# Sliding-window attention and soft mixture of experts on one core: warm products, half loads, moved constants, banks and spreads

## Chip, core and metric

The kernel runs on one core of one Trainium2 chip. The metric is the device time of one execution in microseconds (us). TensorE (PE) multiplies matrices, VectorE (DVE) and ScalarE (ACT) work elementwise, GpSimd (POOL) copies and issues the loads, SyncE (SP) issues the output's transfers.

## What is computed

The input is q, k and v in 8 batches of 8 heads, with 576 positions of 64 values each, and the weights of a soft mixture of 8 experts with 4 slots each. Each position attends to itself and to the 63 positions before it. The result, as 4608 rows of 512 values, goes through the mixture:

```python
scores = q @ k.T / sqrt(64)                      # per batch and head
mask = (rel >= 0) & (rel < 64)                   # rel = query position - key position
attn = softmax(where(mask, scores, -1e9))
x = (attn @ v) reshaped to (4608, 512)

logits = x @ phi                                 # phi: 512 x 32
d = softmax of logits over the 4608 rows         # dispatch
slot_input = d.T @ x                             # 32 x 512
slot_out[e] = relu(slot_input[e] @ w1[e]) @ w2[e]   # w1: 512 x 1024, w2: 1024 x 512
c = softmax of logits over the 32 slots          # combine
out = c @ slot_out
```

## The kernel before

**Attention.** Two heads make a pair, so there are 32 pairs, 4 to a batch. The loop `for n in range(-1, NP - 1)` has one slot for each n, and in a slot several pairs stand at different stages: the maxima of pair n - 1 (`st_max`, `st_max8`), the products with v of pair n - 3 (`st_av`, L329) and their normalization (`st_norm`, L338 and L339), the turning of pair n's q and pair n + 1's k (`st_transpose`, L256) with the copies that scale them (L263, L268), the scores of pair n - 2 (`st_score`, L305 and L307) with their exponential (L312; block 8 by itself, L318), and the shift that carries the maxima into the next products (`st_shift`, L299 and L300). The order of every engine is written out by hand; the program follows it.

**Mixture, front.** Four pairs complete a batch. The functions `fr_*` then make its logits, a running maximum (L377, L379), the exponential (L393), the dispatch weights turned (`fr_dispatch`, L439) and copied (`fr_dispatch_copy`, L444 and L445), and add to the accumulator acc (`fr_acc`, L462). In the loop this is spread over slots 8 to 11 after the batch's first pair; the dispatch of a batch stands in slots 10, 14, 18, 22, 26 and 30, after `st_norm`. The functions `cb_*` make the combine weights: maximum, difference (on GpSimd, L410), exponential (L416), sum (L422), product (on GpSimd, L430) and turning into `ct_all` (L435).

**Loads.** All loads of q, k, v and the expert weights are cast to 16 bits on the way and issued by GpSimd, in an order laid down by `loads(n)`. Each load has one of eight semaphores, so it is issued only once the load eight places before it has landed. Between the loads GpSimd shifts v by 64 positions (`shift_v`, L160 and L162), which `st_av` reads.

**Memory for products.** TensorE writes to five tiles of the accumulator memory: `a_m`, `a_v` and `a_s` of two banks each, `a_k` and `a_q` of one. The block 8 of a pair's maxima, `m8`, lies in `a_v`; that of its scores, `s8`, in `a_k`.

**Tail.** After the loop the last two pairs and batches are written out step by step. `fill(k, bank)` issues k products whose results are not used. The sums over all batches give a factor `fac`, and acc times `fac` is turned by products with `ss` into the slot inputs `sit` (L664, L665, L668, L672). `first(g, f2)` is a half of the first expert products (L692), `turn_hidden` turns the hidden values (L707), `second(g, fcs)` is the second product (L713) into `op`. `spread(b, copy)` brings the combine weights of batch b into the layout that the output needs, by five products (L733) and one copy (L736). All eight spreads stand before the output loop: 0 to 5 among the expert products, 6 and 7 behind them.

**Output.** 13 turns of one to three rows per partition: products (L796), a copy by ScalarE or VectorE in turn (L797), and a transfer by SyncE (L799).

Of the kernel before, what the change touches and what calls it, by code (L numbers as in the profile page):

```python
# [18 lines left out]
def kernel(  # L19
# [10 lines left out]
    nc = tc.nc  # L30
# [33 lines left out]
    nc.vector.memset(a_q[:, 448:512], -1.0e30)  # L64
# [11 lines left out]
    def load_rows(src, g, tag):  # L76
        t = pin.tile([128, 4, RQ * Dh], FP16, name=tag, tag=tag)
        b, gq = divmod(g, 2)
        nc.gpsimd.dma_start(out=t[0:RP], in_=src[b].rearrange("h (p r) d -> p h (r d)", p=RP)[:, 4 * gq:4 * gq + 4, :])  # L79
        staged[tag, g] = t  # L80
# [82 lines left out]

    load_k(1)
# [11 lines left out]
    qbs = [pqk.tile([128, NB, 2, 64], FP16, name=f"qb{i}") for i in range(NQ)]  # L176
    for t_ in kTs:
        nc.vector.memset(t_[:, 0:64], 0.0)
    for t_ in qbs:
        nc.vector.memset(t_[64:128, :, 0, :], 0.0)  # L180
        nc.vector.memset(t_[0:64, :, 1, :], 0.0)
# [6 lines left out]
    nc.vector.tensor_copy(out=db[64:128, 11:12], in_=ident_h[64:128, 64 + NB:65 + NB])  # L188
    wm = const.tile([128, 5, 128], FP16, name="wm")
# [4 lines left out]
    lh = const.tile([128, NB, 128], FP16, name="lh")  # L194
    nc.vector.tensor_copy(out=lh[0:64], in_=wb[:, :].unsqueeze(1).broadcast_to([64, NB, 128]))
    nc.vector.tensor_copy(out=lh[64:128], in_=db[64:128, 0:NB].unsqueeze(2).broadcast_to([64, NB, 128]))
    nc.vector.tensor_tensor(out=lh[64:128, 0, 0:64], in0=lh[64:128, 0, 0:64],
                            in1=db[64:128, 10:11].broadcast_to([64, 64]), op=ALU.add)
    NR = 2
    rts = [const.tile([128, 128], FP16, name=f"rt{i}") for i in range(NR)]  # L200
    for rt in rts:
        nc.vector.tensor_copy(out=rt[64:128, :], in_=db[64:128, 11:12].broadcast_to([64, 128]))
        nc.vector.tensor_copy(out=rt[0:64, 0:64], in_=ident_h[0:64, 0:64])
        nc.vector.tensor_copy(out=rt[0:64, 64:128], in_=ident_h[0:64, 0:64])
    for i in range(2):
# [14 lines left out]
    def late_constants(part):  # L220
        if part == 1:
            nc.vector.tensor_copy(out=phi_sb, in_=phi_f)
            nc.vector.memset(quarter, 0.0)
            for t in range(4):
# [4 lines left out]
            return  # L229
        nc.vector.tensor_copy(out=ssf, in_=ss)  # L230
        nc.vector.memset(emask, 0.0)
        for g in range(2):
# [10 lines left out]
    nc.vector.memset(nmax[1], 1.0e30)  # L243
    nc.vector.memset(stat, 0.0)
# [6 lines left out]
    def st_transpose(p, tag, tq):  # L251
        src = staged[tag, p // 2]
        h = 2 * (p % 2)
# [11 lines left out]
    def st_copy_q(p):  # L265
        for hf in range(2):
            h = slice(64 * hf, 64 * hf + 64)
            nc.scalar.activation(qbs[p % NQ][h, :, hf, :], turned(a_qh)[h], AF.Copy, scale=QKS)  # L268
# [28 lines left out]
    def st_shift(p):  # L297
        t_ = (a_v if p < NP - 1 else a_m)[64:64 + NB, 1, 384:512]
# [197 lines left out]
    for n in range(-1, NP - 1):  # L496
# [57 lines left out]
        if n in (1, 2):  # L554
            late_constants(n)
# [15 lines left out]

    b, p = B - 1, NP - 1
    loads(NP - 1)
    m8_last = a_k[:, 0:128]
    st_max(p - 1)
    st_max8(p - 1)
# [4 lines left out]
    st_max8_read(p - 1)  # L581
    cb_exp(b - 3)
    st_copy_q(p)
    st_av(p - 3)
    st_norm(p - 3)
    st_score(p - 2)
    st_scores(p - 2, (8,), lambda i: s8)
    st_exp8(p - 2)
    fr_transpose(p - 4)
    fr_transpose_copy(p - 4)  # L590
    st_shift(p - 1)
    st_max(p)
    st_max8(p, m8_last)
    st_max8_read(p, m8_last)
# [4 lines left out]
    st_shift(p)  # L599
# [32 lines left out]
    fill(4, a_v[:, 1, :])  # L632
# [17 lines left out]
    fill(2, a_v[:, 1, :])  # L650
# [6 lines left out]
    fill(5, a_m[:, 1, :])  # L657
    fac = pmo.tile([128, 1], FP32, name="fac")
    nc.vector.reciprocal(fac, mg[:, 4:5])
    nc.vector.tensor_tensor(out=fac, in0=fac, in1=wt, op=ALU.mult)  # L660

    accs = [kTs[i][:, 0:256].rearrange("p (c x) -> p c x", c=2) for i in range(2)]
    accv = acc[:, :].rearrange("p (x c) -> p c x", c=NKK)
    nc.vector.tensor_scalar(out=accs[0], in0=accv[:, 0:2, :], scalar1=fac[:, :], scalar2=None, op0=ALU.mult)  # L664
    nc.scalar.activation(accs[1], accv[:, 2:4, :], AF.Copy, scale=fac[:, :])  # L665
    sit_ps = a_q[:, 0:128].rearrange("p (c s) -> p c s", s=32)
    for kk in range(NKK):
        nc.tensor.matmul(sit_ps[:, kk, :], accs[kk // 2][:, kk % 2, :], ss[:, 0, :], start=True, stop=True,  # L668
                         skip_group_check=True)
    fill(2, a_m[:, 1, :])  # L670
    sit = pmo.tile([128, NKK, 32], FP16, name="sit")
    nc.scalar.copy(out=sit, in_=sit_ps)  # L672
    patt.close()
    pex = ExitStack()
# [35 lines left out]
    def second(g, fcs):  # L710
        for fc in fcs:
# [5 lines left out]

    NE = 2 * S // 128
    ct4 = [v1s[0][:, 12 * i:12 * i + 12, :].rearrange("p c x -> p (c x)").rearrange("p (e x) -> p e x", e=NE)
           for i in range(3)]  # L720
    ct4.append(v2s[0][:, :, :].rearrange("p c x -> p (c x)")[:, 0:2 * S].rearrange("p (e x) -> p e x", e=NE))

    ss4 = qbs[2][:, 0:4, :, :].rearrange("p t l x -> p t (l x)")
# [104 lines left out]
```

## Time and profile before

| | us |
|---|---|
| median of 3 runs | 205.19 (204.86 to 205.47) |
| profiled execution | 204.57 |
| its span, first to last instruction | 202.5 |
| TensorE busy in the span | 167.7 (83%) |
| ScalarE busy | 141.2 (70%) |
| VectorE busy | 139.4 (69%) |
| GpSimd busy | 100.4 (50%) |

HBM read was 61.93 MB and written 9.44 MB. Busy time is that of an engine's own instructions; matrix products overlap, so a busy TensorE is not one at its peak. A row of the timeline gives start, duration, engine, line, operation, what it writes and reads, and in brackets the idle time of its engine before it with what ended it. Lines are those of the kernel before.

### The profile page before, as it was taken

The page shows a single profiled execution, that of the slowest core. Times are in us where ns is not written, and L with a number is a line of the kernel's source. Part 1 is how long each engine was busy: PE and PEld are TensorE (multiplying, and loading weights), DVE is VectorE, ACT ScalarE, POOL GpSimd, SP SyncE. Part 2 cuts the span into 40 slices and gives each one's busy share as a digit, 9 for nine tenths or more (in the row PEclk, how much of TensorE's full clock was granted, in tenths as well). Part 3 has the DMA queues.
Part 4 walks back from the last instruction along what each step waited for, and adds up shares of the span by engine and source line. Part 5 has one row for each costly group of instructions (what it writes and reads, how often), then busy time and mean ns, then how long its engine had stood idle before and what let it go on. Part 6 is the DMA issues. An engine that isn't in the chain of part 4 may idle for free.

```text
span 202.5 us, 6749 instructions
## 1 busy us (share of the span) xinstructions
PE 167.7 (83%) x2921; PEld 120.1 (59%) x2921; DVE 139.4 (69%) x328; ACT 141.2 (70%) x255; POOL 100.4 (50%) x127
## 2 busy tenths in 40 slices
PE   0699799989999999999999999999799999555200
PEld 0368677767677677767767776776684355221000
DVE  6878765768676767968777796877677768366300
ACT  2447688879688878969887996988677364465300
POOL 7957837473829655693938674683620024000000
PEclk9999999999999999999999999999999999999965
DMA  5999999999999999999999999999999700199994
GB/s 67 183 182 201 205 199 204 182 205 193 212 190 207 190 213 184 190 210 190 209 187 211 190 211 186 194 208 197 210 214 211 153 18 0 52 394 404 416 419 183
DMA packets 56429, 40.87 MB, mean 202 GB/s; under 512 B 38736, under 2 KB 51024, under 8 KB 55504
## 3 DMA queue, kind: packets, MB, share of 16 engines
q0 software_dynamic: 54000, 30.94, 108.5%
q1 hardware_dynamic: 2400, 9.50, 11.7%
q8 instruction: 23, 0.38, 0.7%
q14 instruction: 6, 0.05, 0.1%
HBM read 61.93 MB, written 9.44 MB: 352 GB/s over the span
## 4 chain that ended last, share of the span: by engine, by line
PE 47%; ACT 18%; DVE 17%; issue 7%; DMA 3%; POOL 2%; DVEq 0%; ACTq 0%; POOLq 0%
ACT qb L268 6%; DVE m L284 6%; PE a_m L279 5%; PE a_m L282 5%; ACT pt L312 4%; PE a_q L256 4%; DVE w L797 4%; PE a_q L353 4%; PE a_s L305 3%; PE a_k L256 3%; PE a_s L307 3%; PE a_v L329 3%; PE cp L796 3%; DMA qs<-in_q_dram 3%; ACT kT L263 2%
## 5 line engine op out<-in xcount | busy, mean ns | idle before, releaser
L268 ACT ACTIVATE qb<-a_q 64x576 f16<-64x576 f16 x64 | 41.2, 644 | 19.6 <-PE a_q L256 19.1
L284 DVE TENSOR_REDUCE m<-a_m 128x8 f16<-128x1024 f32 x32 | 39.2, 1224 | 13.1 <-PE a_m L282 12.6
L312 ACT ACTIVATE pt<-a_s 128x1024 f16<-128x1024 f32 x32 | 32.7, 1023 | 3.3 <-PE a_s L307 2.5
L339 DVE TENSOR_TENSOR x_b<-a_v,rc 128x640 f16<-128x640 f32 x31 | 25.6, 824 | 1.1
L263 ACT ACTIVATE kT<-a_k 128x576 f16<-128x576 f16 x32 | 21.0, 655 | 4.9 <-PE a_k L256 4.8
L153 POOL DMA_DIRECT2D v<-in_v_dram x16 | 19.8, 1235 | 7.5 <-DMA ks<-in_k_dram 5.9
L282 PEld LDWEIGHTS <-qb 128*128 128x128 f16 x256 | 17.6, 101 | 8.6 <-ACT qb L268 1.3
L357 ACT COPY xt<-a_q 128x576 f16<-128x576 f16 x31 | 20.5, 660 | 0.2 <-PE a_q L353 0.2
L307 PEld LDWEIGHTS <-kT 128*128 128x128 f16 x288 | 19.1, 99 | 2.2 <-issue 2.1
L282 PE MATMUL a_m<-kT,qb 128*128 128x128 f16 x256 | 20.4, 225 | 0.0
L305 PE MATMUL a_s<-rt,lh 128*128 128x128 f16 x256 | 20.2, 223 | 0.0
L279 PE MATMUL a_m<-wm,ident_h 128*128 128x512 f16 x64 | 20.2, 399 | 0.0
L256 PE MATMUL a_k<-ident_h,ks 96*64 96x96 f16 x384 | 15.0, 217 | 6.1 <-DMA ks<-in_k_dram 6.1
L307 PE MATMUL a_s<-qb,kT 128*128 128x128 f16 x256 | 19.8, 221 | 0.0
L160 POOL COPY v<-v 64x1152 f16<-64x1152 f16 x16 | 18.2, 1140 | 2.7 <-DMA v<-in_v_dram 2.0
L79 POOL DMA_DIRECT2D qs<-in_q_dram x16 | 11.1, 691 | 16.9 <-PE a_q L256 6.7
L300 DVE CAST rt<-a_v 9x128 f16<-9x128 f32 x31 | 9.0, 289 | 15.0 <-PE a_v L299 14.9
L305 PEld LDWEIGHTS <-lh 128*128 128x128 f16 x288 | 17.9, 99 | 1.8
L162 POOL COPY v<-v 64x1088 f16<-64x1088 f16 (+1 forms) x16 | 17.9, 1118 | 0.8
L256 PE MATMUL a_q<-ident_h,qs 96*64 96x96 f16 x384 | 15.3, 214 | 2.8 <-DMA qs<-in_q_dram 0.8
L329 PE MATMUL a_v<-v,pt 128*64 128x65 f16 x558 | 15.6, 197 | 1.9 <-DVE m L295 1.0
L256 PEld LDWEIGHTS <-ks 96*64 96x64 f16 x384 | 10.7, 115 | 9.9 <-DMA ks<-in_k_dram 6.1
(154 smaller groups left out, 312.5 us busy)
## 6 DMA issues: line engine op xcount, KB each, us to landing
w<-in_moe_w_dram POOLq DMA_DIRECT2D x13, 1024.0 KB, 18.5
out_dram<-w SPq DMA_DIRECT2D x11, 768.0 KB, 7.9
ks<-in_k_dram POOLq DMA_DIRECT2D x16, 288.0 KB, 16.0
qs<-in_q_dram POOLq DMA_DIRECT2D x16, 288.0 KB, 15.4
v<-in_v_dram POOLq DMA_DIRECT2D x16, 288.0 KB, 17.3
w2h<-in_moe_w_dram POOLq DMA_DIRECT2D x4, 256.0 KB, 15.9
w1h<-in_moe_w_dram POOLq DMA_DIRECT2D x4, 256.0 KB, 17.9
w<-in_moe_w_dram POOLq DMA_DIRECT2D x2, 512.0 KB, 15.1
```

Of the source, the lines that this page charges most:

```text
L256: nc.tensor.transpose(tq[64 * hf:64 * hf + 64, RP * r:RP * r + RP], src[0:RP, h + hf, Dh * r:Dh * r + Dh], ident_h[0:RP, 0:RP])
L263: nc.scalar.activation(kTs[p % NK][:, 64:64 + S], turned(a_kh), AF.Copy, scale=QKS)
L268: nc.scalar.activation(qbs[p % NQ][h, :, hf, :], turned(a_qh)[h], AF.Copy, scale=QKS)
L279: nc.tensor.matmul(a_m[:, j, :], ident_h[:, :], wm[:, j:j + 4, :].rearrange("p c x -> p (c x)"), start=True, stop=False, skip_group_check= ...
L282: nc.tensor.matmul(a_m[:, i // 4, 128 * (i % 4):128 * (i % 4) + 128], qblock(p, i), kwindow(p, i), start=False, stop=True, skip_group_chec ...
L284: nc.vector.reduce_max(m[:, 0:8].rearrange("p (l c) -> p l c", l=2), a_m[:, :, :].rearrange("p l (c x) -> p l c x", x=128), axis=AXX)
L305: nc.tensor.matmul(at(i), lh[:, i, :], rt[:, :], start=(i % 4 == 0), stop=False, skip_group_check=True)
L307: nc.tensor.matmul(at(i), kwindow(p, i), qblock(p, i), start=False, stop=True, skip_group_check=True)
L312: nc.scalar.activation(pt[:, 0:8, :].rearrange("p i x -> p (i x)"), a_s[:, :, :], AF.Exp, scale=XS)
L329: nc.tensor.matmul(a_v[r0:r0 + 64, hf, 65 * (i // 2):65 * (i // 2) + 65], pt[:, i, 64 * hf:64 * hf + 64], rhs, start=True, stop=True, skip ...
L339: nc.vector.tensor_tensor(out=xbs[b][:, :, 128 * hp:128 * hp + 128].rearrange("p c (l d) -> p l c d", l=2), in0=avv[:, :, :, 0:64], in1=rc ...
L357: nc.scalar.copy(out=xts[b][:, hp, :], in_=a_qh[:, 0:S])
```

## The change

- `warm_up` issues products of a tile of ones, 10 before the first turning and 6 in slot 0; their results are not used.
- The first group's k and q, loaded as two pairs in one transfer, are loaded one pair a transfer. The second pair's q goes behind the mask constants on GpSimd, and the memset of `wb` moves from VectorE to GpSimd.
- Constants that VectorE made before the loop or in slots 1 and 2 move into slots 1, 2, 5, 7, 15, 19 and 23; two parts of `lh` are made by ScalarE. In pair 0 VectorE makes one of the two copies of q.
- `fr_dispatch` and its copies stand before `st_norm`.
- In the tail, block 8 of the maxima of the last two pairs lies in `a_k`, the shift of pair 30 too, and the steps between are reordered.
- Spreads 0 and 1 stand where a fill product stood in the mixture's tail; 2 and 3 stay among the expert products; 4 to 7 stand in the output loop after turns 4, 6, 8 and 9. Their constant `ss4` is made by GpSimd.
- acc times `fac` is written in acc's own order, in two contiguous halves, and the products read it at stride 4. `op` and the first output row are copied half by ScalarE and half by VectorE.

```diff
-    load_k(0)
-    load_q(0)
+    load_rows(k, 0, "ks", (0,))
+    load_rows(q, 0, "qs", (0,))
     ident_h = const.tile([128, 128], FP16, name="ident_h")
     make_identity(nc, ident_h)
+    load_rows(k, 0, "ks", (1,))
     wb = const.tile([64, 128], FP16, name="wb")
-    nc.vector.memset(wb, 0.0)
+    nc.gpsimd.memset(wb, 0.0)
...
+    warm = v1s[1][:, 0:7, :].rearrange("p c x -> p (c x)")
+    nc.vector.memset(warm, 1.0)
+    def warm_up(n):
+        for i in range(n):
+            nc.tensor.matmul(a_m[:, i % 2, :], warm[:, 0:128], warm[:, 128:640], start=True, stop=True,
+                             skip_group_check=True)
+    warm_up(10)
+    load_rows(q, 0, "qs", (1,))
...
+    def late_constants(n):
+        if n == 1:
+            zero_q(2)
+            ones_v(0)
+        elif n == 2:
+            ones_v(1)
+        elif n == 5:
             nc.vector.tensor_copy(out=phi_sb, in_=phi_f)
...
+        elif n == 7:
             for t in range(4):
                 nc.vector.tensor_copy(out=ss[32 * t:32 * t + 32],
...
+        elif n == 15:
+            nc.vector.tensor_copy(out=ssf, in_=ss)
+            nc.vector.memset(emask, 0.0)
+        elif n in (19, 23):
+            g = n // 4 - 4
             for j in range(4):
...
-        if live(n - 3):
-            st_norm(n - 3)
         if live(n):
             st_transpose(n, "qs", a_qh)
             st_copy_q(n)
+        if n == 0:
+            masks_by_key()
+            warm_up(6)
         if sb is not None:
             fr_dispatch(sb)
             fr_dispatch_copy(sb)
+        if live(n - 3):
+            st_norm(n - 3)
+        if sb is not None:
             fr_stat(sb)
...
-    st_max8(p - 1)
+    st_max8(p - 1, m8k)
     st_transpose(p, "qs", a_qh)
     load_last1()
     shift_v(NG - 1)
     load_w(2 * NRES - 1)
-    st_max8_read(p - 1)
+    make_ss4()
+    st_max8_read(p - 1, m8k)
     cb_exp(b - 3)
     st_copy_q(p)
     st_av(p - 3)
+    st_score(p - 2)
+    st_shift(p - 1, a_k[64:64 + NB, 128:256])
     st_norm(p - 3)
...
-    fill(4, a_v[:, 1, :])
+    spread(0, nc.scalar.copy, a_vf)
+    fill(3, a_k[:, :])
...
-    fill(2, a_v[:, 1, :])
+    spread(1, nc.scalar.copy, a_mf)
+    fill(1, a_v[:, 1, :])
...
-    nc.vector.tensor_scalar(out=accs[0], in0=accv[:, 0:2, :], scalar1=fac[:, :], scalar2=None, op0=ALU.mult)
-    nc.scalar.activation(accs[1], accv[:, 2:4, :], AF.Copy, scale=fac[:, :])
+    nc.vector.tensor_scalar(out=accs[:, 0:256], in0=acc[:, 0:256], scalar1=fac[:, :], scalar2=None, op0=ALU.mult)
+    nc.scalar.activation(accs[:, 256:512], acc[:, 256:512], AF.Copy, scale=fac[:, :])
...
-    nc.scalar.copy(out=osb, in_=op[:, :])
-    cb_turn(b)
-    spread(6, act)
-    spread(7, dve)
+    cb_turn(b)
+    act(out=osb[:, 0:256], in_=op[:, 0:256])
+    dve(out=osb[:, 256:512], in_=op[:, 256:512])
...
+            if turn == 0:
+                act(out=ob[:, 0, 0:256], in_=cp[:, 0, 0:256])
+                dve(out=ob[:, 0, 256:512], in_=cp[:, 0, 256:512])
...
+            if turn in (4, 6, 8, 9):
+                spread((4, 6, 8, 9).index(turn) + 4, (act, dve)[turn % 2])
```

More of the change, by code (lines that the diff above doesn't have):

```diff
@@ L192, with masks_by_key, ones_v @@
     nc.vector.memset(wm[:, 0, 0:64], NEG)
[L194 to L205, printed above, removed]
+    make_rt(rts[1])
+    def masks_by_key():
+        nc.scalar.copy(out=lh[0:64], in_=wb[:, :].unsqueeze(1).broadcast_to([64, NB, 128]))
+        nc.vector.tensor_tensor(out=lh[64:128, 0, 0:64], in0=lh[64:128, 0, 0:64],
+                                in1=db[64:128, 10:11].broadcast_to([64, 64]), op=ALU.add)
+    def ones_v(i):
         nc.vector.memset(v1s[i][:, :, Dh:Dh + 1], 1.0)
@@ L715, in second @@
                                  stop=(g == 1 and fc == NFC - 1), skip_group_check=True)
[L718 to L723, printed above, removed]
[L724 to L737 removed]
     act, dve = nc.scalar.copy, nc.vector.tensor_copy
     first(0, 0)
+    fr_turn(b)
+    cb_max(b - 2)
+    cb_sub(b - 2, nc.gpsimd)
     cb_turn(b - 4)
[L742 to L743 removed]
+    cb_sum(b - 3)
+    cb_mul(b - 3, nc.gpsimd)
     first(0, 1)
[L745 to L746 removed]
+    cb_max(b - 1)
+    cb_sub(b - 1, nc.gpsimd)
     first(1, 0)
     turn_hidden(0)
[L749 to L756 removed]
     cb_exp(b - 2)
@@ L759 @@
     cb_sub(b, nc.gpsimd)
+    first(1, 1)
+    second(0, range(4))
     cb_sum(b - 2)
     turn_hidden(1)
+    spread(2, act)
     cb_mul(b - 2, nc.gpsimd)
+    cb_turn(b - 3)
     cb_exp(b - 1)
-    cb_turn(b - 3)
+    second(0, range(4, 8))
     spread(3, act)
-    second(0, range(4, 8))
     cb_sum(b - 1)
@@ L770 @@
     cb_turn(b - 2)
-    spread(4, act)
-    second(1, range(4))
+    second(1, range(8))
     cb_sum(b)
```

129 lines of the change are left out of this document (66 added, 63 removed).

## The prediction

> **What bounds the kernel now.** I read the page first, then the waits, the chain in order of time, and the timeline around each place the change touches.
>
> ```profile
> span 202.5 us, 6749 instructions
> q0 software_dynamic: 54000, 30.94, 108.5%
> ```
>
> The profiled execution took 204.57 us, so 2.07 us lie around its span. The queue of GpSimd's loads moved 30.94 MB, and its packets took 108.5% of sixteen engines' whole span although loads run for only four fifths of it. The engines are therefore full from the first loads to the last, and a load lands when the bytes ahead of it are through, not when a buffer is free.
>
> ```profile
> PE a_v L329 <- POOL v L162: 0.6, 1, 0.6
> DVE m L284 <- PE a_m L282: 12.6, 23, 0.7
> ```
>
> Behind its load issues GpSimd shifts v (L160, L162), and TensorE once stood 0.6 us at L329 for that shift. What holds GpSimd itself, and how close another slot comes, the timeline shows:
>
> ```profile
> 104.18 0.74 POOL L79 DMA_DIRECT2D qs<-in_q_dram  x1 [2.98 <-DMA w<-in_moe_w_dram]
> 104.97 1.14 POOL L160 COPY v<-v 64x1152 f16<-64x1152 f16 x1
> 106.17 1.09 POOL L162 COPY v<-v 64x1088 f16<-64x1088 f16 x1
> ...
> 107.61 0.47 PE L329 MATMUL a_v<-v,pt 128*64 128x65 f16 x17
> ```
>
> A weight's landing releases the q load at 104.18, the shift ends at 107.26, and L329 needs it at 107.61. So whatever is gained before this slot, no more than 0.35 us of it passes. I call this the pin. The change leaves the bytes and GpSimd's order as they are.
>
> After the loop the chain runs through TensorE, ScalarE and VectorE up to the first output; from there the output's own transfers set the end:
>
> ```profile
> 178.00:200.00 22.00, 6.71 (x27) 2.43 (x26) 8.29 (x5) 7.19 (x5) 0.00 (x0) 0.87 1.00 406
> ```
>
> The DMA share is 1.00 at 406 GB/s while VectorE and ScalarE are busy 8.29 and 7.19 of 22 us. The end moves with the first output, almost one for one.
>
> **The change part by part**
>
> *Start and constants: nothing beyond the pin.* The chain of the first 25 us, by line:
>
> ```profile
> by line: DMA qs<-in_q_dram 21.7%; issue 14.4%; DVE m L284 10.8%; DVE ss L225 6.7%; PE a_m L279 6.0%; PE a_m L282 5.8%; ACT qb L268 5.2%; DVE emask L236 4.7%; PE a_q L256 4.0%; DVE x_b L339 3.3%; PE a_v L299 3.0%; DVE m L295 2.8%; DVE rt L30
> ```
>
> The constants ss and emask, which leave slots 1 and 2, are 11.4% of it, 2.8 us; half loads bring the first pair about 0.75 us sooner (half of the 1.50 us between two landings, below). Warm products and the split copy of q add to a lead of some 3.6 us. The two extra loads, the memset of wb and the sixteen products cost nothing for the same reason: they precede the pin, and full DMA engines cover them. Were that cover gone, two issues of some 0.7 us would show. emask (4.7%, 1.15 us) returns as two halves of 0.6 in slots 19 and 23; VectorE stands 0.55 us on average before L284 (12.6 in 23 waits), which hides them but for 0.1 us.
>
> *Dispatch copies before the normalization.* One such slot:
>
> ```profile
> 139.29 0.82 DVE L339 TENSOR_TENSOR x_b<-a_v,rc 128x640 f16<-128x640 f32 x1
> ...
> 140.17 0.16 DVE L445 COPY dT<-a_k 64x32 f16<-64x32 f16 x1
> ...
> 140.38 0.22 PE L305 MATMUL a_k<-rt,lh 128*128 128x128 f16 x1 [0.23 <-DVE dT L445]
> 140.38 0.10 PEld L307 LDWEIGHTS <-kT 128*128 128x128 f16 x1 [0.35 <-issue]
> ```
>
> The copies stand behind L339; ahead of it they are done before TensorE asks. TensorE idles 0.23, its loads 0.35; with the pipelined tail I take 0.4 a slot. Six slots have it, four before the pin. From the loop I keep 0.35 passed at the pin and 2 x 0.4, less emask's 0.1: **1.1 us** (0.3 if only the pin's share holds, 2.4 for six slots with no pin). The normalization is now queued behind the two copies and their wait for TensorE's transposes, together about 0.5 us; its reader, a transpose one slot later, does not notice.
>
> *Banks of the last pairs.*
>
> ```profile
> 144.71 0.50 PE L329 MATMUL a_v<-v,pt 128*64 128x65 f16 x18 [1.03 <-DVE m L295]
> ...
> 147.23 0.27 ACT L318 ACTIVATE pt<-a_k 128x128 f16<-128x128 f32 x1
> ```
>
> L329 waits 1.03 us for a reduction that reads other columns of a_v. With the max block in a_k the wait goes. What is late next: the last pair's max block now follows the exponential of block 8, also in a_k, so TensorE waits there for a matmul (0.22) and that exponential (0.27), some 0.5. I take 1.03 - 0.5 = **0.5 us** (0 to 1.03). The Trainium skill, "PSUM — Partial Sum Buffer", section "PSUM bank collisions raise a hardware error", says accesses of two engines are kept apart by bank and quadrant, not by address. The 1.03 us wait on other columns agrees; by addresses alone the gain would be 1.03 and the sum 0.5 better.
>
> *Spreads 0 and 1 in place of two fills, and acc.*
>
> ```profile
> 154.58 0.64 ACT L357 COPY xt<-a_q 128x576 f16<-128x576 f16 x1 [0.19 <-PE a_q L353]
> ...
> 156.39 0.42 ACT L393 ACTIVATE d<-a_s,nmax 128x192 f16<-128x192 f32 x1 [1.17 <-DVE nmax L379]
> ...
> 159.59 0.75 ACT L665 ACTIVATE kT<-acc,fac 128x256 f16<-128x256 f32 x1 [1.78 <-DVE fac L660]
> 159.59 0.44 DVE L664 TENSOR_SCALAR kT<-acc,fac 128x256 f16<-128x256 f32 x1
> ```
>
> ScalarE's copy of spread 0 (0.65) fits into the 1.17 us before L393 except that its products must come first: xt is copied by 155.22, then come the logits' products (some 0.3) and the spread's (0.41, below), so the copy runs from about 155.95 to 156.6 and L393 starts 0.2 late: **-0.2** (-0.65 to 0). Spread 1's copy falls into ScalarE's idle time before 159.59. GpSimd prepares ss4 behind its last load issue, microseconds before use; if it came late, its four copies and memset, less elements than one shift, would show at most 1.1 us (L160). acc is read contiguously instead of at stride 4; ScalarE's 0.75 comes down towards VectorE's 0.44: **+0.25** (0 to 0.5).
>
> *Expert stage.* Pieces of the chain that leave this stage:
>
> ```profile
> 162.15 0.36 PE rp L733 x5
> ...
> 163.49 0.36 PE rp L733 x5
> ...
> 169.27 0.41 PE rp L733 x5
> ...
> 170.66 0.36 PE rp L733 x5
> 171.01 1.01 PE op L713 x16
> ```
>
> The four rp pieces are together 1.49; the two spreads that stay each sit up to 0.1 worse: **1.35 us** (1.2 to 1.5).
>
> *First output.* Of the rows around op's end:
>
> ```profile
> 169.10 0.38 ACT L416 ACTIVATE ec<-lgT 128x192 f32<-128x192 f32 x1
> ...
> 170.00 0.36 DVE L435 STREAM_TRANSPOSE ct_all<-cc 128x192 f16<-128x192 f16 x1
> ...
> 170.23 0.51 POOL L430 TENSOR_TENSOR cc<-ec,rs 128x192 f16<-128x192 f32 x1 [0.28 <-DVE rs L423]
> ...
> 172.04 0.58 ACT L779 CAST qb<-op 128x512 f16<-128x512 f32 x1 [1.69 <-PE op L713]
> 172.53 0.65 ACT L736 CAST v<-rp 128x576 f16<-128x576 f32 x1
> ...
> 174.48 0.81 PE L796 MATMUL cp<-qb,v 128*128 128x512 f16 x3 [0.85 <-DVE v L736]
> ...
> 174.95 0.58 ACT L797 COPY w<-cp 128x512 f32<-128x512 f32 x1 [1.78 <-PE cp L796]
> 175.38 1.22 DVE L797 COPY w<-cp 128x1024 f32<-128x1024 f32 x1 [0.95 <-PE cp L796]
> 175.56 16.75 SPq L799 DMA_DIRECT2D out_dram<-w  x13
> ```
>
> Now 3.5 us pass from op's end (172.04) to the first output (175.56); from the copy of op (172.62) to the first row's products (174.48) 1.9 of them go to spreads 6 and 7. After: half copies of op (0.4, against 0.58 whole), 0.47 from product to copy (174.48 to 174.95), half copies of the row (0.4): 1.3. But VectorE's half copy is queued behind the last transposition of weights, L435. Behind spread 3's products now stand two runs of op's (1.01 each), and ahead of the last exponential L416 stand spread 3's copy (0.65) and its own 0.38: it ends 1.0 before op, where it now ends at 169.48, 2.6 before. Then follow sum and reciprocal (0.75, from 169.48 to L430's start), L430 (0.51) and L435 (0.36): 1.6, so VectorE is free some 0.7 late. So 2.0 instead of 3.5, **1.5 us** (0.9 if that wait doubles, 2.2 without it). VectorE's 1.22 us copy of the second output now starts behind its half of the first: **-0.2** (-0.5 to 0). Spreads 4 to 7 beside the output cost ScalarE three copies of 0.65 and VectorE one, in engines two thirds idle; were that cover gone, 2.6 us.
>
> Sum: 1.1 + 0.5 - 0.2 + 0.25 + 1.35 + 1.5 - 0.2 = 4.3. The profiled execution would go to 200.3; it lies 0.62 below the median 205.19, so the median goes to **200.9**.
>
> **The rivals**
>
> *The pin does not hold.* The lead of 3.6 us carries on and six dispatch slots add 2.4. The next stop is the last w1h load:
>
> ```profile
> 143.98 0.54 POOL L132 DMA_DIRECT2D w1h<-in_moe_w_dram  x1 [1.46 <-PE a_q L256]
> ...
> 163.79 0.39 PE L692 MATMUL ha<-w1h,sit 128*32 128x512 f16 x1
> ```
>
> ```profile
> DMA to landing us min/median/max: 15.0/17.9/19.5
> ```
>
> The second answer is that of the tile w1h: no such load lands within 15.0 us of its issue, so this one not before 159.0. It is first read at 163.79: a lead of 4.8 at most. 4.8 + 1.35 + 1.5 - 0.2 = 7.4: 197.8. For it: the waits show L329 held by the shift only once. Against: the full engines. Chance 0.15.
>
> *Loop and tail give nothing*, because a landing a little later eats the 0.35 and each removed wait has another behind it: 1.35 + 1.5 - 0.2 = 2.65 remain: 202.5. Chance 0.16.
>
> *As that, and the output copies fall behind by the four spread copies* (2.6): 205.1, no change. Against: the busy sums of the output window. Chance 0.04.
>
> *Slower: each extra load holds the stream for its fixed part.*
>
> ```profile
> 1.30 0.87 POOL L79 DMA_DIRECT2D ks<-in_k_dram  x1 [0.85 <-POOLq L812]
> ...
> 6.13 0.69 PE L256 MATMUL a_k<-ident_h,ks 96*64 96x96 f16 x12 [6.13 <-DMA ks<-in_k_dram]
> ...
> 7.63 0.69 PE L256 MATMUL a_q<-ident_h,qs 96*64 96x96 f16 x12 [0.81 <-DMA qs<-in_q_dram]
> ```
>
> The first load took 4.83 us, its equal behind it only 1.50 more, so 3.3 are not bytes. If two more loads held the stream 3.3 each, every landing, and through the pin the loop, would come 6.6 later: 207.5. It decides from 4.3 us of delay on. Against: the q load had its own 3.3 too, and it lay under the k load's. The Trainium skill, "DMA: Bandwidth & Descriptors", section "Anatomy of one DMA — SWDGE (gpsimd) path", gives a fixed cost of about 2.0 us a DMA, mostly completion latency; by that estimate twice 2.0 would take the sum to 0.3 and the time to 204.9. The 1.50 us between the landings speaks for latency that overlaps. Chance, with what else could go that way, 0.06.
>
> **How the numbers follow.** The forecast has 0.59; its own range, by the bounds of the terms that are unlikely to fall together, is 199.3 to 202.3. The 8-in-10 range reaches to both neighbours, 197.8 and 202.5, with a little beyond the slower: 197.6 to 203.0. A measurement tells about 0.3%, 0.6 us. Faster: 0.59 + 0.15 + 0.16 = 0.90; same 0.04; slower 0.06.
>
> **What would show it.** Right: the reductions L284 lead by some 3 us around 20 us, by less than 1 us near 107, with waits of TensorE for the shift of v in slots 4 to 9; op's last product near 169, the first output some 2 us behind it, VectorE's half of op waiting for L435. Wrong: a lead over 2 us past 107 (the pin), landings of the first loads more than 1 us later than now (slower), gaps in the DMA share after the first outputs (copies behind).

## The result and the profile after

The changed kernel takes 201.85 us (median of 4 runs, 201.41 to 202.57) where the kernel before takes 205.05 (4 runs beside it, 204.86 to 205.47): a ratio of 0.984, 95% interval 0.981 to 0.988. The forecast was 200.9, with 197.6 to 203.0 as its range. The gain is 3.2 us instead of 4.3. The profiled execution took 202.18 us.

From the page of the changed kernel, the span, GpSimd's queue, and the share of the span by engine in the chain that ended last; below it that share in the kernel before:

```profile
span 200.4 us, 6786 instructions
q0 software_dynamic: 54032, 30.94, 110.0%
DMA 46%; PE 15%; POOL 13%; ACT 7%; issue 6%; DVE 5%; POOLq 0%; DVEq 0%
```

```profile
PE 47%; ACT 18%; DVE 17%; issue 7%; DMA 3%; POOL 2%; DVEq 0%; ACTq 0%; POOLq 0%
```

The same bytes are moved, and the chain, which went through TensorE, ScalarE and VectorE, now goes through transfers and GpSimd. First the loop. The reduction of the maxima (L318, before L284) marks where a pair stands; here are the third reduction in the kernel before and in the changed one, then that of pair 30, the last but one, in both:

```profile
19.61 1.23 DVE L284 TENSOR_REDUCE m<-a_m 128x8 f16<-128x1024 f32 x1
```

```profile
16.02 1.22 DVE L318 TENSOR_REDUCE m<-a_m 128x8 f16<-128x1024 f32 x1 [0.22 <-PE a_m L316]
```

```profile
143.23 1.22 DVE L284 TENSOR_REDUCE m<-a_m 128x8 f16<-128x1024 f32 x1 [0.69 <-PE a_m L282]
```

```profile
144.52 1.23 DVE L318 TENSOR_REDUCE m<-a_m 128x8 f16<-128x1024 f32 x1 [0.70 <-PE a_m L316]
```

A lead of 3.6 us at the start has become a lag of 1.3 at the end of the loop. It was gone early: the changed kernel is 2.8 ahead at the fifth reduction (24.33 against 27.15), 0.3 behind at the sixth (31.58 against 31.32) and 1.5 behind at the eighth. What ate it stands in TensorE's waits, given as line, releaser, total us, times, longest (before: 0.6, 1, 0.6):

```profile
PE a_v L362 <- POOL v L165: 6.3, 6, 1.9
```

Six times, at 17, 26, 36, 47, 91 and 136 us, the product with v waits for the shift of v, which is queued behind load issues: the loop runs at the pace of the loads. And the loads are late. Three stretches of the kernel before and of the changed one, with the DMA share and GB/s as the last two columns:

```profile
5.00:8.00 3.00, 1.06 (x22) 0.88 (x24) 2.84 (x7) 0.65 (x1) 3.00 (x5) 1.00 1.31 193
0.00:20.00 20.00, 12.77 (x181) 9.48 (x182) 16.32 (x62) 9.27 (x14) 15.76 (x26) 1.00 1.32 158
20.00:140.00 120.00, 115.06 (x2243) 89.05 (x2241) 89.32 (x193) 102.28 (x191) 76.75 (x88) 1.00 1.43 199
```

```profile
5.00:8.00 3.00, 3.00 (x31) 1.48 (x30) 1.68 (x7) 1.07 (x2) 3.00 (x4) 1.00 0.90 100
0.00:20.00 20.00, 16.73 (x223) 10.32 (x223) 12.80 (x43) 12.33 (x17) 16.36 (x28) 1.00 1.25 140
20.00:140.00 120.00, 112.51 (x2187) 87.10 (x2185) 89.30 (x207) 99.14 (x185) 76.86 (x89) 0.99 1.43 199
```

From 20 to 140 us the rate is 199 GB/s in both: what is missing at 20 us is never made up. (158 - 140) x 20 us is 0.36 MB, 1.8 us of that rate; most of it falls between 5 and 8 us, 93 GB/s x 3 us = 0.28 MB. This is no accident of two profiles: of the fourteen kernels of this document, the five with half loads moved 92 to 146 GB/s between 5 and 8 us and 139 or 140 in the first 20 us, the nine with whole loads 186 to 196 and 151 to 159.

GpSimd's own rows show a part of it. The first load behind the first group's, in the kernel before and in the changed one:

```profile
3.98 0.68 POOL L79 DMA_DIRECT2D ks<-in_k_dram  x1
```

```profile
5.48 0.68 POOL L79 DMA_DIRECT2D ks<-in_k_dram  x1
```

GpSimd issues it 1.50 us later: two more issues of 0.65 stand ahead of it and the memset of `wb`, 0.22. The first weight load behind them is issued 1.50 later too (11.95 against 10.45) and lands 1.0 later (27.54 against 26.53); the last load of all lands 1.6 later (165.4 against 163.8).

Then the tail. Pair 31's block of maxima waits for one exponential now, and the way from op's end to the first output reads:

```profile
148.18 0.22 PE L325 MATMUL a_k<-wm,ident_h 128*128 128x128 f16 x1 [0.37 <-ACT pt L351]
...
170.76 0.37 ACT L818 CAST qb<-op 128x256 f16<-128x256 f32 x1 [0.95 <-PE op L778]
171.11 0.38 DVE L468 STREAM_TRANSPOSE ct_all<-cc 128x192 f16<-128x192 f16 x1 [0.44 <-POOL cc L463]
171.41 0.38 DVE L819 CAST qb<-op 128x256 f16<-128x256 f32 x1
...
172.26 0.37 ACT L835 COPY w<-cp 128x256 f32<-128x256 f32 x1 [1.13 <-PE cp L833]
172.67 0.42 DVE L836 COPY w<-cp 128x256 f32<-128x256 f32 x1 [0.87 <-ACT w L835]
```

The 1.03 us wait is gone, the new one is 0.37; VectorE's half of op starts 0.65 after ScalarE's, and VectorE's half of the first row waits for ScalarE's half. The first output is issued at 173.12 instead of 175.56, and from there the output takes 25.9 us in both.

### The profile page after: what moved, and what is told of

The parts are those of the page before. It is cut to its first block, busy times and chain, and to the rows that moved or that the text cites. A ratio compares the mean times of both kernels' runs of the same rounds, so it can differ in the third digit from the quotient of the medians.

```text
span 200.4 us, 6786 instructions
## 1 busy us (share of the span) xinstructions
PE 169.1 (84%) x2935; PEld 120.3 (60%) x2935; DVE 135.7 (68%) x322; ACT 143.6 (72%) x258; POOL 103.7 (52%) x135
## 4 chain that ended last, share of the span: by engine, by line
DMA 46%; PE 15%; POOL 13%; ACT 7%; issue 6%; DVE 5%; POOLq 0%; DVEq 0%
DMA w<-in_moe_w_dram 27%; DMA v<-in_v_dram 10%; DMA ks<-in_k_dram 9%; DVE w L838 4%; POOL v L165 3%; POOL v L163 3%; PE cp L833 2%; POOL qs L79 2%; ACT qb L302 2%; POOL ks L79 2%; PE ha L757 2%; POOL v L156 2%; ACT pt L345 1%; PE a_q L286 1%; PE a_s L338 1%
## 5 line engine op out<-in xcount | busy, mean ns | idle before, releaser
L302 ACT ACTIVATE qb<-a_q 64x576 f16<-64x576 f16 x63 | 40.7, 646 | 23.0 <-PE a_q L286 22.6
L318 DVE TENSOR_REDUCE m<-a_m 128x8 f16<-128x1024 f32 x32 | 39.2, 1224 | 12.5 <-PE a_m L316 12.0
L372 DVE TENSOR_TENSOR x_b<-a_v,rc 128x640 f16<-128x640 f32 x31 | 25.6, 824 | 1.1
L362 PE MATMUL a_v<-v,pt 128*64 128x65 f16 x558 | 16.2, 197 | 6.8 <-POOL v L165 6.3
L79 POOL DMA_DIRECT2D qs<-in_q_dram x17 | 11.7, 686 | 16.3 <-PE a_q L286 7.6
L316 PE MATMUL a_m<-kT,qb 128*128 128x128 f16 x256 | 19.7, 221 | 0.0
L362 PEld LDWEIGHTS <-pt 128*64 128x64 f16 x576 | 13.2, 110 | 10.3 <-issue 6.7
L286 PE MATMUL a_q<-ident_h,qs 96*64 96x96 f16 x384 | 14.7, 209 | 1.6
L79 POOL DMA_DIRECT2D ks<-in_k_dram x17 | 11.7, 691 | 7.8 <-DMA w<-in_moe_w_dram 3.0
```

Source lines behind the costliest of these rows:

```text
L79: nc.gpsimd.dma_start(out=t[0:RP, 0:nh, :], in_=src[b].rearrange("h (p r) d -> p h (r d)", p=RP)[:, h0:h0 + nh, :])
L316: nc.tensor.matmul(a_m[:, i // 4, 128 * (i % 4):128 * (i % 4) + 128], qblock(p, i), kwindow(p, i), start=False, stop=True, skip_group_chec ...
L318: nc.vector.reduce_max(m[:, 0:8].rearrange("p (l c) -> p l c", l=2), a_m[:, :, :].rearrange("p l (c x) -> p l c x", x=128), axis=AXX)
L362: nc.tensor.matmul(a_v[r0:r0 + 64, hf, 65 * (i // 2):65 * (i // 2) + 65], pt[:, i, 64 * hf:64 * hf + 64], rhs, start=True, stop=True, skip ...
L372: nc.vector.tensor_tensor(out=xbs[b][:, :, 128 * hp:128 * hp + 128].rearrange("p c (l d) -> p l c d", l=2), in0=avv[:, :, :, 0:64], in1=rc ...
```

## The experiments

Each ran on the chip beside the kernel before (medians 205.07 to 205.64); "gain" is the difference of the two medians. A ratio is the recorded one, with its 95% interval; it need not be the quotient of the two medians.

**The parts alone.** Three parts, each put into the kernel before: the tail as from `fill` on, the dispatch copies ahead of `st_norm`, and the start (half loads, products, moved constants).

The tail (the lines ahead of the cut are the kernel before's, those behind it the changed kernel's, and `st_shift` takes its bank as an argument):

```diff
+    st_max8(p - 1, m8k)
...
+    spread(0, nc.scalar.copy, a_vf)
...
+    act(out=osb[:, 0:256], in_=op[:, 0:256])
+    dve(out=osb[:, 256:512], in_=op[:, 256:512])
```

> The kernel before with the tail alone: banks of the last pairs, spreads, acc, halves of op, output. Theory 'hole': all of the gain sits here, the reduction of pair 30 stays at 143.2 within 0.3, and the time is faster by 3.4 to 4.0 us (3.7 in the trace of after: first output 2.4 earlier, less the 1.3 us that its loop was late). Rival 'engines': part of the gain comes from the loop, so this alone gives 2.5 us or less.

Measured: 201.88 us, ratio 0.982 (0.979 to 0.985), a gain of 3.3 (3.7 by the ratio), where I expected 3.4 to 4.0. The tail makes the whole gain of the change. The other half of what I expected failed: pair 30's reduction, with the kernel before's own loop, came 1.0 later than in the kernel before.

```profile
144.24 1.22 DVE L284 TENSOR_REDUCE m<-a_m 128x8 f16<-128x1024 f32 x1 [0.70 <-PE a_m L282]
```

In this profile the first load landed at 6.50 us instead of 6.08, and 152 GB/s were moved in the first 20 us instead of 158. So the marks of the loop can differ by 1 us between executions of the same code, and one pair of profiles does not show a lag of 1.3 by itself. Over all kernels, pair 30's reduction stands at 144.0 to 144.6 in the five with half loads, at 143.0 to 144.2 in the four with the kernel before's start or one that only adds products to it, and at 140.2 to 142.9 in the five with whole loads in the changed kernel (two of them with the weight loads moved). Only the first and the last group are clear of each other.

The dispatch copies:

```diff
-        if live(n - 3):
-            st_norm(n - 3)
...
             fr_dispatch_copy(sb)
+        if live(n - 3):
+            st_norm(n - 3)
```

> The kernel before with the dispatch copies ahead of the normalization alone. Theory 'hole' (the loop stands on the loads): of 0.4 us in each of six slots only what comes behind the last slot held by the shift of v passes, 0.8 to 1.2 us faster. Rival 'engines': six times 0.4, 2.0 to 2.4 us faster. Third possibility, the copies never were on the path: within 0.3 us of before.

Measured: 204.71 us, 0.997 (0.995 to 0.999), a gain of 0.5, less than the 0.8 to 1.2 expected. The removed idle time of six slots (0.4 each, 2.4) does not pass: pair 30's reduction comes at 142.96 instead of 143.23. TensorE's waits for the shift of v rise from 0.6 to 2.6 us, and two of them show where the time goes:

```profile
107.32 0.35 PE L329 MATMUL a_v<-v,pt 128*64 128x65 f16 x11 [0.27 <-POOL v L162]
134.04 0.35 PE L329 MATMUL a_v<-v,pt 128*64 128x65 f16 x10 [0.90 <-POOL v L162]
```

Before the first of them the reductions lead by 0.77 (106.83 against 107.60), behind it by 0.34 (111.08 against 111.42). The next dispatch slot brings 0.4 again, and the second wait takes it: a lead of 0.73 (133.08 against 133.81) becomes a lag of 0.12 (137.83 against 137.71). The loop stands on the loads already before the change.

The start:

```diff
+    load_rows(k, 0, "ks", (0,))
+    load_rows(q, 0, "qs", (0,))
...
+    warm_up(10)
...
+        late_constants(n)
```

> The kernel before with the start alone: half loads, products, moved constants. Theory 'hole': the load stream loses about 1.5 us while GpSimd makes masks between half loads, the loop stands on the loads, so the reduction of pair 30 comes 1.0 to 1.8 us later than the 143.2 us of before and the time is slower by 1.0 to 1.6 us, although the third reduction comes 3 to 4 us earlier. Rival 'engines': the loop runs at the engines' pace, the lead of the third reduction is kept at least in part, time faster by 1 us or more.

Measured: 205.31 us, 0.999 (0.998 to 1.001): no change, where I expected a loss. The loop did lose what I expected (pair 30 at 144.64, first output issued at 176.98, 1.4 later than before), but the last landing is only 0.2 later (201.68 against 201.46): the output, from its first issue to its last landing, took 24.7 us instead of 25.9. What shortened it is found below.

**Whole first loads** in the changed kernel:

```diff
-    load_rows(k, 0, "ks", (0,))
-    load_rows(q, 0, "qs", (0,))
+    load_k(0)
+    load_q(0)
...
-    load_rows(k, 0, "ks", (1,))
...
-    load_rows(q, 0, "qs", (1,))
```

> After with the first group's k and q loaded whole, ahead of the mask constants, all else as in after. Theory 'hole': the landings go back to those of before, the reduction of pair 30 comes 1.5 to 2.4 us earlier than in after (144.5), the time is 1.3 to 2.4 us less than after, 4.5 to 5.6 less than before. Rival 'engines': the first pair lands 1.5 us later and the time is the same as after's or up to 1 us more.

Measured: 200.25 us (199.64 to 200.43), 0.974 (0.972 to 0.977), 1.6 less than the changed kernel. Its windows and pair 30:

```profile
5.00:8.00 3.00, 1.30 (x28) 0.64 (x25) 2.02 (x7) 0.65 (x1) 3.00 (x4) 0.99 1.28 196
0.00:20.00 20.00, 15.72 (x204) 9.38 (x204) 12.04 (x42) 11.36 (x16) 16.28 (x28) 0.91 1.32 158
```

```profile
142.21 1.23 DVE L316 TENSOR_REDUCE m<-a_m 128x8 f16<-128x1024 f32 x1 [0.69 <-PE a_m L314]
```

The missing bytes are back, and the loop is 1.0 us ahead of before instead of 1.3 behind: 2.3 between the two profiles, 1.6 between the medians. The half loads cost the stream what the change lost in the loop.

**Half loads issued ahead of the masks.** Is it the order on GpSimd, or the halves themselves?

```diff
     load_rows(k, 0, "ks", (1,))
+    load_rows(q, 0, "qs", (1,))
+    load_k(1)
+    load_q(1)
...
-    load_rows(q, 0, "qs", (1,))
-    load_k(1)
-    load_q(1)
```

> The changed kernel, but with the second half loads of k and q and the next pair's whole loads issued before GpSimd builds the wb masks; the loads are cut in halves as before. Hole theory (GpSimd's masks between the half loads let the DMA engines run empty around 5 to 8 us, and every later landing stays late): no slice under 150 GB/s around 5 to 8 us, the third reduction as early as in the changed kernel, the reduction of pair 30 at 142 to 143.4 instead of 144.5, and 0.6 to 1.6 us less than the changed kernel. Rival (the two extra loads themselves hold the stream, wherever they stand): the landings stay 1.2 us or more later than in the kernel before, and the time stays within 0.4 us of the changed kernel.

Measured: 201.15 us, 0.980 (0.978 to 0.982), against the changed kernel's 0.981 to 0.988: 0.7 lower by the medians, but the intervals overlap. Pair 30's reduction is at 144.04, not at the expected 142 to 143.4. Its windows:

```profile
5.00:8.00 3.00, 3.00 (x45) 1.47 (x43) 1.08 (x4) 1.82 (x3) 2.86 (x6) 1.00 1.10 146
0.00:20.00 20.00, 16.69 (x216) 10.43 (x217) 12.49 (x42) 11.62 (x17) 15.64 (x27) 0.91 1.25 140
```

Only half of the hole between 5 and 8 us closes, and at 20 us as much is missing as in the changed kernel (140 GB/s). By the landings (the next k load at 11.08 us against 9.63 in the kernel before, though issued 0.6 later only) the rival was right: the two extra loads hold the stream wherever they stand. The masks between them are not the cause, or not all of it. What this edit can't take away is GpSimd's time for the two extra issues: the first load of v is issued at 6.80, as in the changed kernel (6.81), and at 5.31 in the kernel before. How much of the loss is this issue time, and why two half loads fill the DMA engines less than one whole load, stays open.

**Without the products** in the changed kernel:

```diff
-    nc.vector.memset(warm, 1.0)
...
-    warm_up(10)
...
-            warm_up(6)
```

> The changed kernel without its sixteen warming products and the memset they read. Stream theory (the loop stands on the landings, and an early lead is lost there): TensorE's first transposes and max products at half the speed, as in the kernel before, third reduction 0.5 to 1.5 us later, but the reduction of pair 30 and the time within 0.4 us of the changed kernel. Rival (the lead carries): at least 0.8 us slower. TensorE's instruction count falls by 32, so its code fetch of 16 KB that fell at 178.6 us, inside the output, should fall some 4 us later, still inside the output, and change nothing by that.

Measured: 202.33 us (201.45 to 204.16), 0.988 (0.984 to 0.991). Pair 30's reduction is at 144.44 against 144.52, so the products bring the loop nothing. (Without them even the first reduction comes earlier, at 9.58 instead of 10.17.) The median is 0.5 above the changed kernel's, with intervals that overlap: a small difference is not settled.

**op ahead of the last turning of weights:**

```diff
-    cb_turn(b)
     osb = qbs[0][:, 0:4, :, :].rearrange("p i l x -> p (i l x)")
     act(out=osb[:, 0:256], in_=op[:, 0:256])
     dve(out=osb[:, 256:512], in_=op[:, 256:512])
+    cb_turn(b)
```

> The changed kernel with the two half copies of op ahead of the last transposition of weights, so that VectorE's half no longer waits for GpSimd's product. The forecast priced that wait at 0.7 us; in the trace VectorE's half starts 0.65 us after ScalarE's. If it is on the path to the end: first output 0.5 to 0.7 us earlier, and 0.4 to 0.7 us less than the changed kernel. Rival (ScalarE's half, the products' weights or the output's transfers set the end anyway): within 0.2 us of it.

Measured: 201.69 us, 0.983 (0.980 to 0.985): 0.2 less, not 0.4 to 0.7. The timeline says why:

```profile
170.60 0.37 ACT L817 CAST qb<-op 128x256 f16<-128x256 f32 x1 [0.95 <-PE op L778]
171.00 0.42 DVE L818 CAST qb<-op 128x256 f16<-128x256 f32 x1 [0.49 <-ACT qb L817]
```

With the turning out of the way, VectorE's half waits for ScalarE's half. The two halves of one row in one bank of the accumulator memory are not read side by side in this program, neither here (0.49 us) nor at the first output row (0.87 us).

**More TensorE instructions at the start.** The last landing of the kernel before, and of the changed one, comes 1.3 to 1.5 us after the rest of the output. The windows of the last 2 us of the kernel before, and the queues during its output (packets, MB, share):

```profile
197.50:199.50 2.00, 0.00 (x0) 0.00 (x0) 0.00 (x0) 0.00 (x0) 0.00 (x0) 0.50 1.03 421
199.50:201.50 2.00, 0.00 (x0) 0.00 (x0) 0.00 (x0) 0.00 (x0) 0.00 (x0) 0.50 0.10 40
```

```profile
q1 hardware_dynamic: 1872, 9.44, 87.8%
q8 instruction: 1, 0.02, 0.2%
```

The queue `q8` carries one 16 KB packet of code in the midst of the output, at 185.02 us, and it holds one DMA engine for 0.9 us; at the end the share falls to 0.10, as if one of sixteen engines had work left. Such packets come throughout the run, with some 260 recorded products and weight loads of TensorE between the last two in both kernels, so I took them for TensorE's code. All fourteen profiles bear this out: each has 23 such packets, and the last of them comes after 5809 to 5838 recorded products and weight loads of TensorE, whatever stands ahead. In the kernel with whole first loads the packet came at 176.4 us. This edit to it adds 72 TensorE instructions ahead:

```diff
-    warm_up(10)
+    for i in range(46):
+        nc.tensor.matmul(a_m[:, i % 2, 0:96], warm[:, 0:128], warm[:, 128:224], ...)
```

> The changed kernel with whole first loads (run before as the kernel with whole first loads, 200.25 us), and at the start 46 products of 96 columns in place of 10 of 512: about as many columns, 72 more TensorE instructions. Code theory: a fetch of 16 KB of TensorE's code every 256 of its instructions takes one DMA engine about 1 us; at 176.4 us it fell into the output, and the last landing came 1.5 us after the rest of the output because one engine was late. 72 instructions more bring the fetch before the first output: the last 2 us of the output without a straggler (no slices of 8 to 31 GB/s at its end), output phase 24.3 to 24.8 us instead of 25.7, and 1.0 to 1.4 us less than the kernel with whole first loads, 198.9 to 199.3. Rival (the straggler has another cause, such as the order of the writes): output phase 25.5 or more and the time within 0.3 us of 200.25.

Measured: 199.06 us (198.43 to 199.30), 0.970 (0.967 to 0.972), 1.2 less than with ten products. The packet now falls at 168.1 us, and the output takes 24.7 us instead of 25.7, although it starts 0.7 later in this profile.

The same 46 products in the kernel before, with nothing else changed:

> The kernel before with 46 small products (96 columns) on a filled tile at the start, while TensorE waits for the first load: nothing else is changed. They are 92 TensorE instructions, which bring the fetch of TensorE's code from 185.0 us, 9.5 us into the output, to ahead of the first output. Code theory: output phase 24.6 to 24.8 us instead of 25.9 and 0.9 to 1.3 us less than before. Rival (the products act by TensorE's clock at the start, or not at all): output phase still 25.6 or more; the third reduction earlier than 19.0 us, yet the time within 0.4 us of before, since the loop stands on the loads.

Measured: 204.09 us (12 runs) against 205.21, 0.995 (0.993 to 0.997), 1.1 less. Pair 30's reduction is 0.8 later than before in the profiles, so the loop is not where it comes from; the output takes 24.6 us. (The two profiles are only 0.5 apart, because that of the kernel before lies 0.6 under its median here.) Queues during its output, and the last 2 us of the landings:

```profile
q1 hardware_dynamic: 1872, 9.44, 87.7%
```

```profile
199.00:201.00 2.00, 0.00 (x0) 0.00 (x0) 0.00 (x0) 0.00 (x0) 0.00 (x0) 0.50 0.72 295
```

No code packet, and no late engine: the share stays full until shortly before the last landing at 200.98. This also explains the start alone: its 32 extra instructions brought the packet to 176.95 us, just ahead of the first output's issue (176.98), which gave back 1.2 of the 1.4 lost in the loop. In the changed kernel the packet lies inside the output again (178.56), so there the loss shows. Over the fourteen profiles the two groups do not touch: with the last packet inside the output, the output takes 25.6 to 26.2 us (eight kernels), with the packet ahead of it 24.6 or 24.7 (six).

**Whole copies of op and of the first row** by ScalarE, in the kernel with the 46 products:

```diff
-    act(out=osb[:, 0:256], in_=op[:, 0:256])
-    dve(out=osb[:, 256:512], in_=op[:, 256:512])
+    act(out=osb, in_=op)
...
-            if turn == 0:
-                act(out=ob[:, 0, 0:256], in_=cp[:, 0, 0:256])
-                dve(out=ob[:, 0, 256:512], in_=cp[:, 0, 256:512])
-            else:
-                (act, dve)[turn % 2](out=ob[:, 0:ne, :], in_=cp[:, 0:ne, :])
+            (act, dve)[turn % 2](out=ob[:, 0:ne, :], in_=cp[:, 0:ne, :])
```

> The kernel with whole first loads and 46 small products (199.06 us), with op and the first output row each copied whole by ScalarE in place of a half by ScalarE and a half by VectorE. In the trace VectorE's half waits for ScalarE's both times, so the halves take 0.82 us (row) and 1.03 us (op) where one whole copy took 0.58 in the kernel before. If that is the path: first output 2.4 us after op's end comes down to about 1.75, and the time falls by 0.5 to 0.7 us, to 198.4 to 198.6. Rival (the output's transfers or the second row's copy by VectorE set the end anyway): within 0.2 us of 199.06.

Measured: 198.18 us (197.90 to 198.95), 0.965 (0.962 to 0.968), 0.9 less, where 0.5 to 0.7 were expected.

```profile
168.69 0.59 ACT L818 CAST qb<-op 128x512 f16<-128x512 f32 x1 [0.95 <-PE op L778]
169.33 0.81 PE L832 MATMUL cp<-qb,v 128*128 128x512 f16 x3 [0.69 <-ACT qb L818]
169.74 0.59 ACT L833 COPY w<-cp 128x512 f32<-128x512 f32 x1 [0.46 <-PE cp L832]
170.23 1.22 DVE L833 COPY w<-cp 128x1024 f32<-128x1024 f32 x1 [0.81 <-PE cp L832]
170.36 1.46 SPq L835 DMA_DIRECT2D out_dram<-w  x2
```

One copy of 0.59 each, and 1.67 us from the start of op's copy to the first output, where the halves needed 2.36 in the changed kernel and 2.15 with op ahead of the turning.

**Weight loads one slot later**, without and with the whole copies:

```diff
-    WSLOTS = {5 * i // 2: i for i in range(13)}
+    WSLOTS = {5 * i // 2 + 1: i for i in range(13)}
```

> The same kernel (199.06 us) with every expert-weight load of the loop issued one slot later (slots 1, 3, 6, 8, ... in place of 0, 2, 5, 7, ...), so that each stands behind one more k, v or q load of the loop. Stream theory (the loop waits for v and q landings behind 1 MB of weights): the waits of TensorE for the shift of v and for q loads fall from 3.7 us in all to under 2, the reduction of pair 30 comes 0.5 to 1.5 us earlier and the time falls by 0.4 to 1.2 us. Rival (the bytes ahead of the last landings are the same, and the expert stage waits for the last weights instead): new waits of TensorE for DMA in the expert stage, the same time within 0.3 us or up to 1 us more.

> Both: whole copies of op and the first row by ScalarE, and the weight loads one slot later. If both effects are real and independent their sum: 0.9 to 1.9 us less than 199.06. If the weights then land too late, the whole copies alone: 0.5 to 0.7 us less, or nothing.

Measured: 197.11 us (196.87 to 198.08), 0.960 (0.957 to 0.964), without, and 196.78 us (196.39 to 197.43), 0.958 (0.954 to 0.961), with the whole copies: 2.0 and 1.4 less than their counterparts. The second kernel is the fastest found, 5.1 us under the changed one. The mechanism is half shown. With the whole copies TensorE's waits for the shift of v fall from 2.8 us to 1.5 and pair 30 comes 1.1 earlier (141.34 against 142.47); without them they fall from 2.9 to 2.5 only, and most of that profile's lead (17.00 against 19.33 at the third reduction) comes from the start, where its products ran faster (last section). The whole copies, worth 0.9 before, are worth 0.3 here, within the scatter.

## Why the prediction was nearly right

The steps of the profiled executions, forecast and measured. The marks are pair 30's reduction, pair 30's scores (147.69 before, 148.29 after), the exponential L393 (156.39, 156.95), the first expert product (161.10, 161.56), the copy of op (172.04, 170.76) and the first output (175.56, 173.12).

| term | forecast | measured |
|---|---|---|
| loop, to pair 30's reduction | +1.1 | -1.3 |
| banks, to pair 30's scores | +0.5 | +0.7 |
| spread 0's copy, to L393 | -0.2 | 0.0 |
| acc, to the first expert product | +0.25 | +0.1 |
| expert stage, to op's copy | +1.35 | +1.7 |
| first output | +1.5 | +1.2 |
| the output after it | -0.2 | 0.0 |
| sum | 4.3 | 2.4 |

The two profiled executions give 2.4 (204.57 to 202.18); the medians give 3.2. No row tells to which term the 0.8 between them belongs, but the loop's marks are those that scatter most (the tail alone). The medians give the plainest account: the forecast's terms of the tail add up to 3.2, the tail alone gained 3.3 and the whole change 3.2. The loop, forecast at +1.1, gave nothing.

That the time still fell into the range is in part luck: the loop's term fell outside its own bounds (0.3 to 2.4), while the errors of the tail's terms, up to 0.4 each in the profiles, nearly cancelled by the medians.

**The step that failed is that the two extra loads "cost nothing", because "they precede the pin, and full DMA engines cover them".** It rests on "The change leaves the bytes and GpSimd's order as they are", which was wrong: the change puts two more loads and the memset of `wb` among GpSimd's first issues and one q load behind the masks. The reason holds only if the engines stay full, and they did not: at 5 to 8 us, where the two extra loads stand, they moved 100 GB/s instead of 193. The pin, which I used to argue that an early gain is lost, also passes an early loss of the stream to the end. I applied it in one direction only. The price for the case that the cover is gone, "two issues of some 0.7 us", comes near: the rows above show 1.50 us of later issues, and the runs price the half loads at 1.6 (whole loads against halves, medians). The "slower" rival had 6.6 us for two loads, from its reading that 3.3 of the first load's 4.83 us "are not bytes". That reading does not hold. The shortest times from issue to landing among the k loads, which belong to the first load, in the kernel before and in the changed one:

```profile
DMA to landing us min/median/max: 4.8/16.0/19.5
```

```profile
DMA to landing us min/median/max: 3.3/16.2/18.8
```

Half the bytes took 1.5 us off, so by a straight line through the two (an estimate) only some 1.8 are not bytes. By the Trainium skill ("DMA: Bandwidth & Descriptors", "Anatomy of one DMA — SWDGE (gpsimd) path"), which gives about 2.0 us of fixed cost for one DMA, the estimate was 4.0. The 1.8 is near that page's figure, and the measured 1.6 lies between nothing and the 4.0; no run here separates how much of it is a load's fixed time and how much GpSimd's time to issue it.

**The pin was right as a mechanism, but it is not one slot.** The dispatch copies alone gained 0.5 of a possible 2.4: the wait at 107 let 0.34 through, as read (0.35), but I counted 2 x 0.4 behind it as gained, and a second wait at 134 took most of that. With whole loads the loop gains 1.0 in the profiles, against the 1.1 of the forecast. In the changed kernel none of the six waits is at 107; the lead of 3.6 us, forecast and measured, was lost by 40 us. It did not only shrink, as I had put it; with the stream late it turned into a lag.

**Banks** came out as reasoned: a wait of 0.37 for the exponential of block 8 in place of 1.03 (I took 0.5).

**First output:** VectorE's half of op did wait for L435's counterpart, 0.65 (forecast 0.7). Its sum was short because I let the halves of op and of the first row run side by side, 0.4 each; they run one after the other, 0.37 and 0.42 for the row. I had quoted the rule that speaks against it: the Trainium skill, "PSUM — Partial Sum Buffer", section "PSUM bank collisions raise a hardware error", keeps two engines' accesses to one bank and quadrant apart, reads included. The rows agree (0.87 us, ended by ScalarE's half). I had used it for L329 and not for my own half copies. Once the wait for the turning was gone, this one took its place, which is why that experiment gave 0.2.

**Expert stage:** the four rp pieces were 1.49; 1.7 was measured, so the two spreads that stay did not sit worse by the 0.1 each that I allowed; where the other 0.2 comes from is not shown. The spreads in the output loop were hidden, as forecast: the output took 25.9 us in both.

The rival "loop and tail give nothing" (202.5) came closer to 201.85 than the forecast did (0.65 against 0.95). Its half on the loop, a later landing that eats the gain, is what happened; its half on the tail is not: the removed wait there stayed removed.

## What to carry to other kernels

Where the loop stands on a full stream of loads, price an early edit by the bytes that have landed at a fixed time (two window rows of GB/s), not by the lead of the first instructions: the lead is lost in the loop, a hole in the stream is not. Before splitting a copy over two engines, look which bank both halves read; a whole copy by one engine was 0.5 us shorter over two such steps (2.15 to 1.67). And when a final transfer phase ends with its DMA share at a few hundredths, look for an instruction packet inside that phase; it can be moved by changing the number of instructions ahead of it.

## What the runs showed of the hardware that was not expected

- Packets of 16 KB, taken for TensorE's code by their place in its count of instructions, come over the same DMA engines during the run. One inside the output made the kernel 1.1 to 1.2 us longer (two kernels, with and without).
- Four first loads of one pair each in place of two loads of two pairs cost the changed kernel 1.6 us; a half load's issue took GpSimd 0.65 us, a whole one's 0.69.
- Like code ran at half the pace at the start in one execution and not in the next. The six products in slot 0, in the kernels with 46 products, first without and then with the weight loads one slot later:

```profile
8.26 2.74 PE L172 MATMUL a_m<-v 128*128 128x512 f16 x6
```

```profile
8.27 1.47 PE L172 MATMUL a_m<-v 128*128 128x512 f16 x6
```

They began before the first moved load was issued, with the same work ahead. The granted clock between 8.26 and 11.00 us reads 1.00 in both profiles, so the rows do not show the cause; in the kernel with both edits the same six took 2.74 us at a granted clock of 0.50. The first reduction came at 13.48 and 11.14 us. One look at a profile can thus differ by 2.3 us at the start; medians of several runs were needed to compare such kernels.
